# Fused decay attention and gated feed-forward on one core: block 1's v before the output weights' second half, projection 0's second half inside gate/value 1

## The chip, the cores and the metric

The kernel runs on one core of a Trainium2 chip. The metric is the device time of one execution in microseconds. Engines: TensorE (PE) multiplies matrices, VectorE (DVE), ScalarE (ACT) and GpSimd (POOL) work on tiles, and SyncE (SP), POOL and ACT issue DMAs from their own instruction streams.

## The reference

Inputs are q, k, v of 4 batches, 8 heads, 768 positions and head dimension 64, and a decay lam per head. A causal linear attention with decay runs in blocks along the sequence and carries a 64 x 64 state per batch and head. Its output, 3072 tokens by 512, goes through a gated feed-forward with 1536 inner features:

```python
intra = np.einsum('bhic,bhjc->bhij', qb, kb) * Dmask[None]
intra = np.einsum('bhij,bhjd->bhid', intra, vb)
inter = np.einsum('bhid,bhde->bhie', qb * lam_pow[None], kv_state)
out[:, :, sl] = intra + inter
kb_dec = kb * rev_pow[None]
kv_state = lam_block * kv_state + np.einsum('bhsd,bhse->bhde', kb_dec, vb)
...
gate = 1.0 / (1.0 + np.exp(-(x @ w_gate)))
return (gate * (x @ w_val)) @ w_out
```

## The kernel before, in words

The sequence is cut into six blocks (n = 0 to 5) of 128 positions. A block of all four batches gives 512 tokens. Everything is computed in bf16 with sums in PSUM.

**Attention of a block.** q and k have to lie with the head dimension on the partitions. For blocks 0 and 1 PE transposes them (`t_`, L219), and ACT and DVE evict them into KS and QS (`e_k` L240, `e_q` L226; from block 1 on, QS is also multiplied by powers of lam). From block 2 on, DMA transposes that SP issues do it (`xbar`, L251): kt first, then qt. `piece_s` (L260) computes the scores of one batch into two PSUM tiles, and `piece_m` (L271) multiplies them on DVE with the decay mask into MT. `piece_kd` (L115) makes the decayed keys on ACT, one instruction for each head and half of the batches (for block 0 one per head). `att` (L476) then runs `piece_i` (state times q; it reads Sb), `piece_a` (scores times v, into the same PSUM tiles), `piece_x` (eviction to XT; for blocks 0 and 1 batches 0 and 2 on ACT, 1 and 3 on DVE) and `piece_c` (decayed keys times v, four head pairs in two halves), whose result updates the state Sb on DVE. For block 0 the state was zero, so `piece_c(0)` is simply copied to Sb.

**Feed-forward of a block.** `piece_gv` (L331), called a gate/value step, computes 128 of the 1536 inner features: four matmuls for the gate (gp), a sigmoid on ACT, four matmuls for the value (vp), and a product on DVE into HT. A block has twelve such steps. `piece_po` (L349), the projection, multiplies HT of one batch (tt) with WO in twelve matmuls, evicts to ob (on ACT unless another engine is given) and stores with a DMA issued by SP. The projection of block 0 is done in two halves of 256 columns, of later blocks in one of 512, but for the last one of all.

**Order.** [...] A list, `plan`, holds the feed-forward units in order, and behind each unit stand smaller pieces of attention (`behind` L489 for block 0's gate/value steps, `after` L501 for its projection, `more` L509 for later blocks). In the kernel before, `piece_c(0)` stands behind gate/value step 5 of block 0; the transposes of block 1's batches 0, 1 behind step 8; those of batches 2, 3 behind projection unit 2 of the first half; block 1's kd in four groups behind projection units, the last ahead of `att(1)`, which stands behind unit 2 of the second half. `next_loads(n)` (L441) issues the DMA transposes of block n on SP, two tiny POOL copies that wait for them (`gate`), and the loads of block n's v and of the next block's k and q on POOL. For block 2 it stands behind gate/value step 2 of block 1.

**Loads.** POOL issues nearly all of them, in program order (L163 to L169 and L423 to L433); for a swapped half of the batches, `load` (L83) issues two DMAs. The order around the change is k and q of block 1's batches 2, 3, then WO's second 256 columns, then v of block 1, then k and q of block 2.

**PSUM.** Attention tiles take turns in five buffers (`ps_at`), those of the feed-forward in three (`ps_ff`). Ahead of block 0's feed-forward stand matmuls on zeros (`zeros`, L364) that fill PE's time.

Of the kernel before, what the change touches and what calls it, by code (L numbers as in the profile page):

```python
# [16 lines left out]
def kernel(  # L17
# [11 lines left out]
    nc = tc.nc  # L29

    B, H, S, D = q.shape
# [8 lines left out]
    NB2 = B // 2  # L40
# [30 lines left out]
    def swapped(n, b):  # L71
        return n > 0 and b >= NB2

    def slot(n, b, h):
        return h ^ 1 if swapped(n, b) else h

    def half(b, h):
        return (1 - h % 2) if b >= NB2 else h % 2

    def rows_of(u):  # L80
        return slice(u * 64, (u + 1) * 64)

    def load(n, what, b0=0, b1=B):  # L83
        sl = slice(n * C, (n + 1) * C)
        for c in what:
            if (c, n) not in T_:
                T_[c, n] = qkv.tile([128, B, H, D], BF16, tag=c + "b", name=c + "b",
                                      bufs=5 if c == "v" else 4)
            src = {"q": q, "k": k, "v": v}[c]
            nat = b1 if n == 0 or c == "v" else min(b1, NB2)  # L90
            if b0 < nat:
                nc.gpsimd.dma_start(  # L92
                    out=T_[c, n][:, b0:nat],
                    in_=src[b0:nat, :, sl, :].rearrange("b h s d -> s (b h) d"))
            if nat < b1:
                m = max(nat, b0)
                for u in range(2):
                    nc.gpsimd.dma_start(  # L98
                        out=T_[c, n][:, m:b1, u::2, :],
                        in_=src[m:b1, 1 - u::2, sl, :].rearrange("b h s d -> s (b h) d"))  # L100
# [11 lines left out]
    def make_kd(n):  # L112
        KD[n] = kdp.tile([128, B, H, D], BF16, tag="kd", name="kd")

    def piece_kd(n, hs):  # L115
        for h in hs:
            for bs in ((0, B),) if n == 0 else ((0, NB2), (NB2, B)):
                at = slice(*bs)
                i = slot(n, bs[0], h)
                nc.scalar.mul(KD[n][:, at, i, :], T_["k", n][:, at, i, :], kds[:, h:h + 1])  # L120
# [9 lines left out]
    Sb = stp.tile([128, HP, B, 64], BF16, tag="Sb", name="Sb")  # L130
# [88 lines left out]
    def t_(c, n, bs):  # L219
        ps = ps_at.tile([128, len(bs), HP, C], BF16, name="t" + c, tag="ps")  # L220
        for i, b in enumerate(bs):
            for hp in range(HP):
                nc.tensor.transpose(ps[:, i, hp, :], T_[c, n][:, b, 2 * hp:2 * hp + 2, :], ident)
        (tqs if c == "q" else tks)[n, bs[0]] = ps
# [15 lines left out]
    def e_k(n, bs, parts=1):  # L240
        t = trsb.tile([128, 2, HP, C], BF16, tag="KS", name="KS")
        w = len(bs) // parts
        for i in range(parts):
            nc.scalar.copy(t[:, i * w:(i + 1) * w], tks[n, bs[0]][:, i * w:(i + 1) * w])
        for i in range(len(bs)):
            KS[n, bs[i]] = t[:, i]
# [13 lines left out]
    def piece_s(n, bs):  # L260
        for b in bs:
            sp = [ps_at.tile([128, HP, C], FP32, name=f"sp{u}", tag="ps") for u in range(2)]
            for hp in range(HP):
                for u in range(2):
                    us = slice(u * 64, (u + 1) * 64)
                    nc.tensor.matmul(sp[u][:, hp, :], lhsT=KS[n, b][us, hp, :],  # L266
                                     rhs=QS[n, b][us, hp, :],
                                     start=(hp == 0), stop=(hp == HP - 1), skip_group_check=True)
            SP[n, b] = sp

    def piece_m(n, b):  # L271
        MT[n, b] = mtp.tile([128, 2, HP, C], BF16, tag="MT", name="MT")
        for u in range(2):
            nc.vector.tensor_tensor(out=MT[n, b][:, u], in0=SP[n, b][u],  # L274
                                    in1=(mask if n else mask0)[:, 1 - u if swapped(n, b) else u],
                                    op=ALU.mult)
# [31 lines left out]
    def piece_c(n, hps):  # L308
        cp = ps_at.tile([128, len(hps), B, 64], FP32, name="cp", tag="ps")
        for i, hp in enumerate(hps):  # L310
            for b in range(B):
                for w in range(2):
                    h = 2 * hp + w
                    nc.tensor.matmul(cp[rows_of(half(b, h)), i, b, :],  # L314
                                     lhsT=KD[n][:, b, slot(n, b, h), :], rhs=T_["v", n][:, b, h, :],
                                     start=(i == 0 and b == 0), stop=(i == len(hps) - 1 and b == B - 1),
                                     skip_group_check=True)
        if n == 0:
            nc.vector.tensor_copy(Sb[:, hps[0]:hps[-1] + 1], cp)
            return  # L320
        for i, hp in enumerate(hps):
            for at, d in ((slice(0, NB2), dec), (slice(NB2, B), decs)):
                nc.vector.scalar_tensor_tensor(  # L323
                    out=Sb[:, hp, at, :], in0=Sb[:, hp, at, :], scalar=d[:, hp:hp + 1],
                    in1=cp[:, i, at, :], op0=ALU.mult, op1=ALU.add)
# [38 lines left out]
    def zeros(m):  # L364
        for _ in range(m):
            nc.tensor.matmul(zps, lhsT=Sb[:, 0, 0:2, :], rhs=Sb[:, 0:2], start=True, stop=True)  # L366
# [17 lines left out]
    tables_late()  # L384
    piece_s(0, [0])
    piece_m(0, 0)
    piece_s(0, [1])
    piece_m(0, 1)
    t_("k", 0, [2, 3])
    e_k(0, [2, 3], parts=2)  # L390
    zeros(2)
    t_("q", 0, [2])
    e_q(0, [2], nc.scalar)
# [32 lines left out]
    load(1, "q", 0, 2)  # L426
    load_gv(10, 12)
    load_wo(0, 256)
    load(1, "k", 2, 4)
    load(1, "q", 2, 4)  # L430
    load_wo(256, 512)
    load(1, "v")
    load(2, "kq")  # L433

    gates = const.tile([128, 2], BF16, tag="gates")
# [19 lines left out]
    def gv(n, ft, *more):  # L455
        unit(lambda: piece_gv(n, ft), *more)

    def po(n, tt, *more, c=(0, DM), eng=nc.scalar):
        unit(lambda: piece_po(n, tt, *c, eng), *more)

    def pair(f, n, bp):
        return lambda: f(n, [2 * bp, 2 * bp + 1])

    def m_(n, b):
        return lambda: piece_m(n, b)

    def trans(n, bp):
        def go():
            bs = [2 * bp, 2 * bp + 1]
            t_("k", n, bs)  # L470
            e_k(n, bs)
            t_("q", n, bs)
            e_q(n, bs)
        return go

    def att(n):  # L476
        def go():
            piece_i(n)
            piece_a(n, range(B))
            piece_x(n, range(B))  # L480
            if n < NSTEP - 1:
                piece_c(n, [0, 1])
                piece_c(n, [2, 3])
        return go

    def kd(n, h0):
        return lambda: piece_kd(n, [h0, h0 + 1])

    behind = {ft: [] for ft in range(NFT)}  # L489
    for ft in range(4):  # L490
# [1 line left out]
    behind[0].append(swap_halves)  # L492
    behind[1].append(lambda: make_mask(0))
    behind[3].append(lambda: make_mask(1))
    behind[5] = [pair(piece_c, 0, 0), pair(piece_c, 0, 1)]
    behind[8] = [trans(1, 0)]
    behind[9] = [pair(piece_s, 1, 0), m_(1, 0)]
    behind[10] = [m_(1, 1)]
    for ft in range(NFT):
        gv(0, ft, *behind[ft])  # L500
    after = {(0, 1): [kd(1, 0)], (0, 2): [trans(1, 1)], (0, 3): [pair(piece_s, 1, 1), m_(1, 2), kd(1, 2)],  # L501
             (1, 0): [m_(1, 3), kd(1, 4)], (1, 1): [kd(1, 6)], (1, 2): [att(1)]}
    for j in range(2):
        for tt in range(B):
            po(0, tt, *after.get((j, tt), []), c=(256 * j, 256 * (j + 1)))

    for n in range(1, NSTEP):
        nx = n + 1
        more = [[] for i in range(NFT)]  # L509
        if nx < NSTEP:  # L510
            more[3] = [lambda nx=nx: e_q(nx, [0, 1])]
            more[4] = [pair(piece_s, nx, 0), m_(nx, 0)]
            more[5] = [m_(nx, 1), lambda nx=nx: e_q(nx, [2, 3])]
            more[7] = [pair(piece_s, nx, 1), m_(nx, 2)]
            more[8] = [m_(nx, 3)]
            more[11] = [att(nx)]
        if nx < NSTEP - 1:
            for i in range(4):
                more[6 + i].append(kd(nx, 2 * i))
            more[5].append(lambda nx=nx: make_kd(nx))  # L520
        if n == 1:
            more[4:11] = more[3:10]
            more[3] = []
            more[2].append(lambda: next_loads(2))
            more[8].append(lambda: next_loads(3))
        for ft in range(NFT):
            gv(n, ft, *more[ft])
        for tt in range(B):
            if n == NSTEP - 1 and tt == B - 1:
                po(n, tt, c=(0, 256))  # L530
                po(n, tt, c=(256, 512), eng=nc.vector)
            else:
                more = [lambda n=n: next_loads(n + 3)] if tt == B - 1 and n + 3 < NSTEP else []
                po(n, tt, *more)
# [35 lines left out]
```

## Time and profile before

| | |
|---|---|
| three runs | 229.17, 229.33, 229.39 us; median 229.33 |
| the profiled execution | 229.37 us, its span 227.6 us |
| granted PE clock | 0.997 |
| PE, DVE, ACT, POOL busy | 216.2, 101.6, 100.9, 59.5 us |
| bytes moved by DMA | 25.31 MB |
| gate/value 0 starts on PE | 16.08 us |
| projection 0 starts | 39.30 us |
| gate/value 1 starts | 55.07 us |
| projection 1 starts | 79.29 us |

The profile is one execution with the start and end of each instruction. PE, DVE, ACT and POOL are busy where they work on data; time before an instruction in which its engine stood idle is given with what ended it. DMA issues on POOL and SP are listed with the time from issue to landing. Times are counted from the start of the span, so the profiled execution's own time is 1.77 us more than its last time.

### The profile page before, as it was taken

What the parts mean: (1) busy time and instruction counts of PE and PEld (TensorE: products, weight loads), DVE (VectorE), ACT (ScalarE), POOL (GpSimd) and SP (SyncE); (2) the same over time, 40 slices, a digit from 0 to 9 for tenths busy, and PEclk for the clock granted to TensorE, in tenths of its full rate; (3) what the DMA queues carried; (4) which work ended last, traced back from release to release, by engine and by line L of the source; (5) the groups of instructions that cost most, each with busy time, mean ns of one, the idle gap of its engine ahead of it and who ended that gap; (6) DMA issues with size and microseconds to landing.
All of it is one profiled execution on the core that took longest, in us unless ns stands there. A gap on an engine that the chain in (4) does not pass through costs nothing.

```text
span 227.6 us, 4227 instructions
## 1 busy us (share of the span) xinstructions
PE 216.2 (95%) x1689; PEld 110.9 (49%) x1713; DVE 101.6 (45%) x186; ACT 100.9 (44%) x216; POOL 59.5 (26%) x75
## 2 busy tenths in 40 slices
PE   6689999979999999999999999999999999999994
PEld 1444454867444644444544444554444544444443
DVE  4754657145468620388430378530368600333300
ACT  5767443565337732338532328532333342333221
POOL 7997654700067009302900030000000000000000
PEclk9999999999999999999999999999999999999998
DMA  7999999999939999995995939012100012100022
GB/s 115 147 174 200 193 180 181 194 193 178 212 57 153 147 209 106 207 193 98 109 157 154 192 53 82 0 49 92 46 3 0 0 49 92 46 0 3 0 94 92
DMA packets 106195, 25.31 MB, mean 111 GB/s; under 512 B 94144, under 2 KB 103744, under 8 KB 106176
## 3 DMA queue, kind: packets, MB, share of 16 engines
q0 software_dynamic: 82816, 13.90, 79.3%
q1 hardware_dynamic: 22896, 11.01, 19.5%
q8 instruction: 13, 0.21, 0.4%
q10 hardware_dynamic: 464, 0.14, 0.3%
q14 instruction: 6, 0.05, 0.1%
HBM read 28.32 MB, written 6.29 MB: 152 GB/s over the span
## 4 chain that ended last, share of the span: by engine, by line
PE 77%; DMA 15%; POOL 5%; issue 2%; DVE 0%; POOLq 0%
PE po L354 25%; PE vp L342 23%; PE gp L336 22%; DMA WO<-in_moe_w_out_dram 7%; DMA qb<-in_q_dram 5%; DMA WG<-in_moe_w_gate_dram 3%; PE op L296 2%; PE sp L266 2%; PE op L285 1%; POOL vb L92 1%; POOL kb L92 1%; PE cp L314 1%; POOL WG L104 1%; POOL qb L92 1%; POOL WV L105 1%
## 5 line engine op out<-in xcount | busy, mean ns | idle before, releaser
L345 DVE TENSOR_TENSOR ht<-sg,vp 128x512 bf16<-128x512 bf16 x72 | 49.4, 686 | 94.3 <-PE vp L342 92.7
L342 PE MATMUL vp<-XT,WV 128*128 128x512 bf16 x287 | 73.8, 379 | 0.3
L336 PE MATMUL gp<-XT,WG 128*128 128x512 bf16 x272 | 71.5, 379 | 1.5 <-issue 0.8
L339 ACT ACTIVATE sg<-gp 128x512 bf16<-128x512 f32 x72 | 43.0, 597 | 66.5 <-PE gp L336 63.0
L354 PE MATMUL po<-WO,ht 128*128 128x512 bf16 (+1 forms) x343 | 63.6, 342 | 1.8 <-DMA WO<-in_moe_w_out_dram 1.5
L354 PEld LDWEIGHTS <-ht 128*128 128x128 bf16 x348 | 33.5, 98 | 29.8 <-issue 1.5
L342 PEld LDWEIGHTS <-WV 128*128 128x128 bf16 x288 | 28.2, 98 | 34.0 <-DMA WV<-in_moe_w_val_dram 0.2
L336 PEld LDWEIGHTS <-WG 128*128 128x128 bf16 x288 | 27.3, 98 | 32.4 <-issue 0.3
L357 ACT COPY ob<-po 128x512 f32<-128x512 f32 (+1 forms) x28 | 14.4, 515 | 45.3 <-PE po L354 45.3
L274 DVE TENSOR_TENSOR MT<-sp,mask 128x512 bf16<-128x512 f32 x48 | 30.5, 682 | 1.9 <-PE sp L266 1.9
L120 ACT ACTIVATE kd<-kb,kds 128x128 bf16<-128x128 bf16 (+1 forms) x72 | 23.8, 402 | 0.0
L439 POOL COPY gates<-kt 128x1 bf16<-128x1 bf16 x4 | 0.7, 186 | 54.8 <-DMA kt<-kb 54.8
L306 ACT CAST XT<-op 128x512 bf16<-128x512 f32 x21 | 10.9, 597 | 5.6 <-PE op L296 5.6
L92 POOL DMA_DIRECT2D vb<-in_v_dram x7 | 10.9, 1563 | 1.4 <-issue 0.9
L323 DVE SCALAR_TENSOR_TENSOR Sb<-Sb,dec,cp 128x128 bf16<-128x128 bf16 x32 | 8.6, 342 | 3.3 <-PE cp L314 3.3
L98 POOL DMA_DIRECT2D kb<-in_k_dram x10 | 8.8, 895 | 3.2 <-DMA WO<-in_moe_w_out_dram 2.3
L98 POOL DMA_DIRECT2D qb<-in_q_dram x10 | 8.9, 918 | 1.3 <-DMA kb<-in_k_dram 0.8
L92 POOL DMA_DIRECT2D qb<-in_q_dram x7 | 8.4, 1205 | 0.8 <-POOLq L554 0.8
L366 PE MATMUL zps<-Sb 128*128 128x512 bf16 x19 | 6.5, 469 | 1.6 <-DVE Sb L147 1.5
L92 POOL DMA_DIRECT2D kb<-in_k_dram x6 | 6.9, 1158 | 1.4 <-DMA WV<-in_moe_w_val_dram 0.8
L296 PE MATMUL op<-MT,vb 128*64 128x128 bf16 x184 | 6.5, 221 | 0.0
L296 PEld LDWEIGHTS <-vb 128*64 128x64 bf16 x184 | 5.3, 110 | 1.3 <-issue 0.4
(55 smaller groups left out, 81.9 us busy)
## 6 DMA issues: line engine op xcount, KB each, us to landing
out_dram<-ob SPq DMA_DIRECT2D x19, 256.0 KB, 2.0
vb<-in_v_dram POOLq DMA_DIRECT2D x5, 512.0 KB, 7.0
qb<-in_q_dram POOLq DMA_DIRECT2D x7, 256.0 KB, 8.3
kb<-in_k_dram POOLq DMA_DIRECT2D x6, 256.0 KB, 8.0
WO<-in_moe_w_out_dram POOLq DMA_DIRECT2D x2, 768.0 KB, 14.6
WG<-in_moe_w_gate_dram POOLq DMA_DIRECT2D x5, 256.0 KB, 9.2
WV<-in_moe_w_val_dram POOLq DMA_DIRECT2D x5, 256.0 KB, 9.8
kb<-in_k_dram POOLq DMA_DIRECT2D x10, 128.0 KB, 8.6
```

What stands on the lines that cost most here:

```text
L92: nc.gpsimd.dma_start(out=T_[c, n][:, b0:nat], in_=src[b0:nat, :, sl, :].rearrange("b h s d -> s (b h) d"))
L98: nc.gpsimd.dma_start(out=T_[c, n][:, m:b1, u::2, :], in_=src[m:b1, 1 - u::2, sl, :].rearrange("b h s d -> s (b h) d"))
L120: nc.scalar.mul(KD[n][:, at, i, :], T_["k", n][:, at, i, :], kds[:, h:h + 1])
L274: nc.vector.tensor_tensor(out=MT[n, b][:, u], in0=SP[n, b][u], in1=(mask if n else mask0)[:, 1 - u if swapped(n, b) else u], op=ALU.mult)
L296: nc.tensor.matmul(OP[n, b][rows_of(w), hp, :], lhsT=T_["v", n][:, b, h, :], rhs=MT[n, b][:, slot(n, b, h) % 2, hp, :], start=(n == 0 and ...
L306: (e.tensor_copy if e is nc.vector else e.copy)(XT[n][:, :, b, :], OP[n, b])
L336: nc.tensor.matmul(gp, lhsT=WG[:, mt, fs], rhs=x[:, mt, :], start=(mt == 0), stop=(mt == NMT - 1))
L339: nc.scalar.activation(sg, gp, AF.Sigmoid)
L342: nc.tensor.matmul(vp, lhsT=WV[:, mt, fs], rhs=x[:, mt, :], start=(mt == 0), stop=(mt == NMT - 1))
L345: nc.vector.tensor_mul(HT[n, ft], sg, vp)
L354: nc.tensor.matmul(po[:, :c1 - c0], lhsT=HT[n, ft][:, tt * 128:(tt + 1) * 128], rhs=WO[:, ft, c0:c1], start=(ft == 0), stop=(ft == NFT - 1))
L357: (eng.copy if eng is nc.scalar else eng.tensor_copy)(o, po[:, :c1 - c0])
```

## The change

Five parts. In the prologue of block 0, the PE transposes of k for batches 2, 3 and their eviction come ahead of batch 1's scores. `piece_c(0)` moves from behind gate/value step 5 to behind projection unit 3 of block 0, just ahead of `att(1)`, and its copies to Sb run on ACT instead of DVE. Block 1's k and q of batches 2 and 3 are loaded, transposed and evicted one batch at a time, and v of block 1 is loaded ahead of WO's second half. Of block 1's kd, the half for batches 0, 1 moves behind gate/value steps 10 and 11; the half for batches 2, 3 is eight instructions ahead of `att(1)`. The second half of projection 0 (four units) is done between gate/value steps 1 and 2 of block 1. At the very end, the last 256 columns of the last projection are computed, evicted and stored as two pieces of 128, the first evicted on DVE, the second on ACT.

```diff
--- before.py
+++ after.py
@@ -112,9 +112,9 @@
     def make_kd(n):
         KD[n] = kdp.tile([128, B, H, D], BF16, tag="kd", name="kd")
 
-    def piece_kd(n, hs):
+    def piece_kd(n, hs, parts=(0, 1)):
         for h in hs:
-            for bs in ((0, B),) if n == 0 else ((0, NB2), (NB2, B)):
+            for bs in ((0, B),) if n == 0 else [((0, NB2), (NB2, B))[i] for i in parts]:
                 at = slice(*bs)
                 i = slot(n, bs[0], h)
                 nc.scalar.mul(KD[n][:, at, i, :], T_["k", n][:, at, i, :], kds[:, h:h + 1])
@@ -316,7 +316,7 @@
                                      start=(i == 0 and b == 0), stop=(i == len(hps) - 1 and b == B - 1),
                                      skip_group_check=True)
         if n == 0:
-            nc.vector.tensor_copy(Sb[:, hps[0]:hps[-1] + 1], cp)
+            nc.scalar.copy(Sb[:, hps[0]:hps[-1] + 1], cp)
             return
         for i, hp in enumerate(hps):
             for at, d in ((slice(0, NB2), dec), (slice(NB2, B), decs)):
@@ -384,10 +384,10 @@
     tables_late()
     piece_s(0, [0])
     piece_m(0, 0)
+    t_("k", 0, [2, 3])
+    e_k(0, [2, 3], parts=2)
     piece_s(0, [1])
     piece_m(0, 1)
-    t_("k", 0, [2, 3])
-    e_k(0, [2, 3], parts=2)
     zeros(2)
     t_("q", 0, [2])
     e_q(0, [2], nc.scalar)
@@ -426,10 +426,11 @@
     load(1, "q", 0, 2)
     load_gv(10, 12)
     load_wo(0, 256)
-    load(1, "k", 2, 4)
-    load(1, "q", 2, 4)
+    for b in range(2, 4):
+        load(1, "k", b, b + 1)
+        load(1, "q", b, b + 1)
+    load(1, "v")
     load_wo(256, 512)
-    load(1, "v")
     load(2, "kq")
 
     gates = const.tile([128, 2], BF16, tag="gates")
@@ -464,9 +465,8 @@
     def m_(n, b):
         return lambda: piece_m(n, b)
 
-    def trans(n, bp):
+    def trans(n, bs):
         def go():
-            bs = [2 * bp, 2 * bp + 1]
             t_("k", n, bs)
             e_k(n, bs)
             t_("q", n, bs)
@@ -483,8 +483,11 @@
                 piece_c(n, [2, 3])
         return go
 
-    def kd(n, h0):
-        return lambda: piece_kd(n, [h0, h0 + 1])
+    def kd(n, h0, h1=None, **kw):
+        return lambda: piece_kd(n, range(h0, h1 or h0 + 2), **kw)
+
+    def s_(n, b):
+        return lambda: piece_s(n, [b])
 
     behind = {ft: [] for ft in range(NFT)}
     for ft in range(4):
@@ -492,17 +495,18 @@
     behind[0].append(swap_halves)
     behind[1].append(lambda: make_mask(0))
     behind[3].append(lambda: make_mask(1))
-    behind[5] = [pair(piece_c, 0, 0), pair(piece_c, 0, 1)]
-    behind[8] = [trans(1, 0)]
+    behind[8] = [trans(1, [0, 1])]
     behind[9] = [pair(piece_s, 1, 0), m_(1, 0)]
-    behind[10] = [m_(1, 1)]
+    behind[10] = [m_(1, 1), kd(1, 0, 4, parts=[0])]
+    behind[11] = [kd(1, 4, 8, parts=[0])]
     for ft in range(NFT):
         gv(0, ft, *behind[ft])
-    after = {(0, 1): [kd(1, 0)], (0, 2): [trans(1, 1)], (0, 3): [pair(piece_s, 1, 1), m_(1, 2), kd(1, 2)],
-             (1, 0): [m_(1, 3), kd(1, 4)], (1, 1): [kd(1, 6)], (1, 2): [att(1)]}
-    for j in range(2):
-        for tt in range(B):
-            po(0, tt, *after.get((j, tt), []), c=(256 * j, 256 * (j + 1)))
+    cols = [(256 * j, 256 * j + 256) for j in range(2)]
+    po(0, 0, c=cols[0])
+    po(0, 1, trans(1, [2]), c=cols[0])
+    po(0, 2, s_(1, 2), m_(1, 2), trans(1, [3]), c=cols[0])
+    po(0, 3, s_(1, 3), m_(1, 3), pair(piece_c, 0, 0), pair(piece_c, 0, 1), kd(1, 0, 8, parts=[1]),
+       att(1), c=cols[0])
 
     for n in range(1, NSTEP):
         nx = n + 1
@@ -525,10 +529,14 @@
             more[8].append(lambda: next_loads(3))
         for ft in range(NFT):
             gv(n, ft, *more[ft])
+            if (n, ft) == (1, 1):
+                for tt in range(B):
+                    po(0, tt, c=cols[1])
         for tt in range(B):
             if n == NSTEP - 1 and tt == B - 1:
                 po(n, tt, c=(0, 256))
-                po(n, tt, c=(256, 512), eng=nc.vector)
+                po(n, tt, c=(256, 384), eng=nc.vector)
+                po(n, tt, c=(384, 512))
             else:
                 more = [lambda n=n: next_loads(n + 3)] if tt == B - 1 and n + 3 < NSTEP else []
                 po(n, tt, *more)
```

## The prediction

> **What bounds the kernel now.** I read the page's busy line first, then TensorE's (PE's) timeline, then the timelines of the engines that feed it. The busy line:
>
> ```profile
> PE 216.2 (95%) x1689; PEld 110.9 (49%) x1713; DVE 101.6 (45%) x186; ACT 100.9 (44%) x216; POOL 59.5 (26%) x75
> ```
>
> PE is busy 216.2 of 227.6 us, so a change can win only where PE stands idle, and every new idle stretch is lost in full, since nothing behind it has slack. PE's timeline around the change (start, length, instruction, idle time before it):
>
> ```profile
> 26.57 0.69 PE L314 MATMUL cp<-vb,kd 128*64 128x64 bf16 x32
> ...
> 39.30 4.11 PE L354 MATMUL po<-WO,ht 128*128 128x256 bf16 x36
> ...
> 47.63 4.09 PE L354 MATMUL po<-WO,ht 128*128 128x256 bf16 x36 [1.48 <-DMA WO<-in_moe_w_out_dram]
> 51.66 0.64 PE L285 MATMUL op<-QS,Sb 64*64 64x128 bf16 x32
> 52.23 1.08 PE L296 MATMUL op<-MT,vb 128*64 128x128 bf16 x32
> 53.14 0.67 PE L314 MATMUL cp<-vb,kd 128*64 128x64 bf16 x32
> ...
> 65.52 0.62 PE L266 MATMUL sp<-QS,kt 64*128 64x128 bf16 x16
> ```
>
> The one wait worth removing is 1.48 us at 47.63, for the second half of the output weights (WO). A second gate shows no idle time: WO's first half lands at 39.25 (issued 24.95, 14.3 us to landing), just as PE comes to projection 0 at 39.30. PE cannot start it sooner whatever is taken out of gate/value 0. GpSimd's (POOL's) timeline shows the queue discipline:
>
> ```profile
> 24.95 1.02 POOL L108 DMA_DIRECT2D WO<-in_moe_w_out_dram  x1 [0.39 <-DMA WG<-in_moe_w_gate_dram]
> ...
> 39.54 0.87 POOL L98 DMA_DIRECT2D kb<-in_k_dram  x1 [2.27 <-DMA WO<-in_moe_w_out_dram]
> ```
>
> The load at 39.54 is the eighth after WO's first half and waits for its landing; the other POOL waits here also point eight loads back. ScalarE (ACT), VectorE (DVE) and the SP queue:
>
> ```profile
> 50.84 1.27 ACT L120 ACTIVATE kd<-kb,kds 128x128 bf16<-128x128 bf16 x4
> 52.02 0.35 ACT L357 COPY ob<-po 128x256 f32<-128x256 f32 x1
> 52.68 1.07 ACT L306 CAST XT<-op 128x512 bf16<-128x512 f32 x2 [0.31 <-PE op L296]
> ```
> ```profile
> 64.58 0.69 DVE L233 TENSOR_TENSOR QS<-qt,lamq 128x1024 bf16<-128x1024 bf16 x1
> ```
> ```profile
> 56.17 3.92 SPq L254 DMA_TRANSPOSE kt<-kb  x1
> 60.27 1.89 SPq L254 DMA_TRANSPOSE qt<-qb  x1
> ...
> 125.62 1.90 SPq L254 DMA_TRANSPOSE kt<-kb  x1
> 127.73 2.26 SPq L254 DMA_TRANSPOSE qt<-qb  x1
> ```
>
> kd is done on ACT before attention 1 begins to be evicted. And block 2's transposed q lands at 64.57 (60.27 plus 4.3), DVE takes it at 64.58, PE needs the result at 65.52: this path has about 0.2 us of slack.
>
> [...] The trace agrees (kd, ob and XT above run in program order), and this decides the forecast. [...] The trace has 390 and, from four in 1.27 to 1.28 us, 297. [...] So a transpose queued on SP behind a store waits for that store's eviction; the trace agrees (161.6 us of waits of SP's stores for ob).
>
> **The change part by part.** The sum is against the profiled execution: 229.37 us, span 227.6, 1.77 around it (the median is 229.33). Pitches on PE from the starts above: a 256-column projection of 12 matmuls 1.31 (36 in 3.94); k and q transposes of one batch 0.45; scores of one batch 0.28; piece_i 0.57, piece_a 0.91, piece_c pair 0.61; a gate/value step 1.727.
>
> *Prologue order.* Batches 2, 3 of k are transposed inside a 0.47 us PE gap. QS of batch 2 still waits for q's DMA (PE idle 0.49 at 11.16), so nothing is gained; a loss up to 0.4 would vanish in the next point's slack. 0.
>
> *piece_c of block 0 leaves gate/value 0.* PE would end that stage about 0.6 early and wait at 39.30 for WO. Gain 0. The same work returns after the anchor: +0.61.
>
> *Loads.* Eight small k/q loads replace four, and each POOL issue costs about 0.73 (the price of a load with as few packets, WG's 0.74) against 0.87. The eighth starts at 39.54 behind WO, v at 40.3, WO's second half at 42.0. v takes 6.9 to landing when the queue is empty (the one at 65.25), so it lands at 47.2; WO2 lands 4.95 later (its distance from q's landing before, 42.6 to 47.55), at 52.2. Batch 2's k, q are there by 40.9 (needed 41.9), batch 3's by 43.6 (needed 44.0 to 44.2). The 1.48 goes, and neither v nor WO2 is late, with about 1 and 2.3 us to spare.
>
> *Projection 0, first half, with attention between.* From 39.30: po 0 to 40.61, po 1 to 41.93, transposes to 42.37, po 2 to 43.69, scores 2 to 43.97, transposes to 44.41, po 3 to 45.73. DVE does the mask product of batch 2 from 44.12 (two at a pitch of 0.60) and QS of batch 3 by about 45.72; scores 3 run 45.78 to 46.06, piece_c(0) to 46.67.
> *First new wait.* Until now piece_c(0)'s Sb copies were hidden 25 us ahead; now attention 1 needs them at once. ACT copies Sb from 46.60 (0.22 after its matmuls, as XT does) and, at a pitch of 0.49, has the second at 47.67. DVE's mask product of batch 3 runs 46.21 to 47.50, and piece_i's third matmul needs its PSUM buffer (five, in rotation). piece_i starts at 47.56: 0.9 idle. It ends at 48.17, piece_a at 49.08 (v there at 47.2), the first piece_c half at 49.38.
> *Second new wait.* Behind the Sb copies on ACT stand eight kd, 8 x 0.297 = 2.38, from 47.58 to 49.96, and only then the two XT evictions of batches 0, 2: to 50.54 and 51.04. The second piece_c half needs the last kd and batch 0's PSUM buffer: 50.6. Gate/value 1 needs all of XT: 51.10. Idle 1.2 plus 0.2. Before, 1.32 us of projection covered XT's eviction; that cover is gone. The two kd groups moved into gate/value 0 cost nothing (0.6 + 1.27 us of ACT per 1.73 step, the excess of 0.1 hidden under projection 0).
>
> *Second half inside gate/value 1.* Two steps to 54.55, four projections to 59.80; ACT's evictions (0.37 each per 1.31) are covered. Before, the same work was done at 58.52. So **+1.28**: 1.48 and little else won, 0.61 paid back, 2.3 newly idle.
>
> *What that does to SP.* The first transpose of block 2 stands behind the last of these stores. Before, PE left the projection at 55.07 and kt was issued at 56.17, 1.10 later; now at 60.90. Before, block 2's q landed 8.7 us after the large load ahead of it (51.7 to 60.4), with a transpose crossing; now that makes 60.9 at the latest, so the pair goes through unhindered. The trace has this once, at 125.62: kt's issue to qt's landing 6.9 us. The others took 8.0 to 8.4, with q still loading. I take 6.9: qt lands at 67.8, DVE's QS ends at 68.5, PE's scores of block 2 start at 68.6 rather than 65.52. PE comes there at 59.80 + 4 x 1.727 = 66.7: a **third new wait of 1.9**. After it everything is the old schedule, later by 3.1; block 3's loads and transposes shift along, with 10 us in hand.
>
> *Tail.* The last 256 columns go as two of 128: the final eviction falls from DVE's 0.42 to about 0.26 on ACT (585 and 366 ns at 512 and 256 columns, continued), the store from 128 to 64 KB, unpriced: 0 to 0.3. 24 matmuls at 0.056 (the transposes' pitch) cost 0.02 more. Taken -0.15; ends -0.4 and +0.1.
>
> Sum: scores of block 2 at 68.6 against 65.52 is 3.08 later, that is 1.28 and 1.9 less a gap of 0.1 that was there before: 229.37 + 3.08 - 0.15 = **232.3**.
>
> **Rivals.** *Transposes slow:* the pair takes 8.2, as three of four did, because loads or stores cross it: 233.6. For: it is the commoner value. Against: k and q of block 2 should be in by then. 13%.
> *Only the first wait is real:* ACT's kd do not hold XT (1.4 us less): kt at 59.5, qt at 66.4, scores at 67.2: 230.9. [...] 13%.
> *Faster:* attention stays fed, as it does now at 51.66 to 55.07, because the six evicting steps fit under PE's work. Then PE works 18.1 us through, projection 0 ends at 57.4, 1.1 ahead of before, and with the tail gives 228.1. It decides only if the transposes, issued at 58.5, land within 5.0 us; beyond 6.25 the kernel is slower even so, and the shortest pair seen is 6.9. 5%.
> *v or WO2 late by over 2 us:* above 234. 5%. *Gains and losses cancel:* 229.3. 2%.
>
> **How the numbers follow.** Forecast 62%. The range takes in the two middle rivals: 230.7 to 233.8, some 88%, and part of the forecast's own spread. About 0.2% is what a measurement here can tell from no change; beyond it slower 93%, faster 5%, within it 2%.
>
> **What would show it.** Right: PE's line for WO at 47.63 without a wait; idle before op L285 of about 0.9 and before gate/value 1 of over 1 us with ACT's kd in one row of eight ahead of XT; kt issued near 60.9, QS of block 2 near 67.8 and an idle time of about 1.9 before sp L266. Wrong: XT evicted ahead of kd; kt issued before the last store of projection 0; or qt landing before 65.

## The result, and the profile after

The changed kernel takes 232.48 us (median of 4 runs, 232.10 to 232.85) against 229.35 for the kernel before (4 runs, 229.17 to 229.39): 1.0138 times as long, 95% interval 1.0120 to 1.0156. The forecast was 232.3, range 230.7 to 233.8. The profiled execution of the changed kernel took 232.10 us with a span of 230.3, against 229.37 and 227.6: 2.73 us more.

The busy line of the page after: PE has more busy time than before and the same share. A share of 95% says nothing of where the loss lies. Nor can the two times be subtracted: before, 24 of the 1713 matmuls have no record (1689 beside 1713 weight loads), after, none of 1725.

```profile
PE 219.7 (95%) x1725; PEld 111.6 (48%) x1725; DVE 100.6 (44%) x185; ACT 102.6 (45%) x220; POOL 61.6 (27%) x79
```

PE's timeline after (start, length, instruction, idle time before it and what ended it) shows each place of the forecast:

```profile
39.22 2.79 PE L354 MATMUL po<-WO,ht 128*128 128x256 bf16 x24 [0.67 <-DMA WO<-in_moe_w_out_dram]
...
46.22 0.70 PE L314 MATMUL cp<-vb,kd 128*64 128x64 bf16 x32
47.34 1.02 PE L285 MATMUL op<-QS,Sb 64*64 64x128 bf16 x32 [0.43 <-ACT Sb L319]
48.51 1.08 PE L296 MATMUL op<-MT,vb 128*64 128x128 bf16 x32
49.43 0.98 PE L314 MATMUL cp<-vb,kd 128*64 128x64 bf16 x32
51.12 1.02 PE L336 MATMUL gp<-XT,WG 128*128 128x512 bf16 x4 [0.70 <-ACT XT L306]
...
54.56 5.40 PE L354 MATMUL po<-WO,ht 128*128 128x256 bf16 x48
...
68.59 0.62 PE L266 MATMUL sp<-QS,kt 64*128 64x128 bf16 x16 [1.72 <-DVE QS L233]
```

The old wait of 1.48 us for WO's second half is gone: at 54.56 there is no idle time. In its place stand a wait of 0.67 ahead of projection 0 (most of it the time that piece_c(0) left behind), idle time in and around attention 1, 0.70 before gate/value 1, and 1.72 before the scores of block 2. Waits can also hide inside a line that merges several instructions: the 32 matmuls of piece_i take 1.02 us where they took 0.64, those of piece_c 0.98 where they took 0.67.

ACT's timeline after shows the row that holds XT up: the Sb copies, eight kd, then the evictions to XT.

```profile
46.71 1.07 ACT L319 CAST Sb<-cp 128x512 bf16<-128x512 f32 x2 [0.34 <-PE cp L314]
47.67 2.45 ACT L120 ACTIVATE kd<-kb,kds 128x128 bf16<-128x128 bf16 x8
50.01 1.05 ACT L306 CAST XT<-op 128x512 bf16<-128x512 f32 x2
```

Both transposes on SP's queue, and DVE's use of the result 0.1 us after its landing (63.12 plus 4.6):

```profile
60.91 2.03 SPq L254 DMA_TRANSPOSE kt<-kb  x1
63.12 2.40 SPq L254 DMA_TRANSPOSE qt<-qb  x1
```
```profile
67.85 0.69 DVE L233 TENSOR_TENSOR QS<-qt,lamq 128x1024 bf16<-128x1024 bf16 x1 [1.90 <-DMA qt<-qb]
```

### The profile page after: what moved, and what is told of

It reads as the page before. It is cut to its first block, busy times and chain, and to the rows that moved or that the text cites. A ratio compares the mean times of both kernels' runs of the same rounds, so it can differ in the third digit from the quotient of the medians.

```text
span 230.3 us, 4287 instructions
## 1 busy us (share of the span) xinstructions
PE 219.7 (95%) x1725; PEld 111.6 (48%) x1725; DVE 100.6 (44%) x185; ACT 102.6 (45%) x220; POOL 61.6 (27%) x79
## 4 chain that ended last, share of the span: by engine, by line
PE 76%; DMA 15%; POOL 3%; ACT 2%; issue 1%; SPq 1%; DVE 0%; POOLq 0%; DVEq 0%; ACTq 0%
PE po L354 27%; PE gp L336 21%; PE vp L342 21%; DMA WO<-in_moe_w_out_dram 6%; DMA WG<-in_moe_w_gate_dram 4%; DMA vb<-in_v_dram 3%; PE sp L266 2%; DMA qt<-qb 2%; PE op L296 2%; ACT kd L120 1%; PE op L285 1%; SPq L254 1%; PE cp L314 1%; POOL qb L92 1%; POOL vb L92 1%
## 5 line engine op out<-in xcount | busy, mean ns | idle before, releaser
L336 PE MATMUL gp<-XT,WG 128*128 128x512 bf16 x288 | 74.0, 379 | 1.1 <-ACT XT L306 0.7
L354 PE MATMUL po<-WO,ht 128*128 128x512 bf16 (+2 forms) x360 | 63.9, 337 | 0.7 <-DMA WO<-in_moe_w_out_dram 0.7
L357 ACT COPY ob<-po 128x512 f32<-128x512 f32 (+2 forms) x29 | 14.8, 509 | 47.8 <-PE po L354 47.8
L98 POOL DMA_DIRECT2D qb<-in_q_dram x12 | 10.2, 864 | 5.8 <-DMA WO<-in_moe_w_out_dram 3.7
L98 POOL DMA_DIRECT2D kb<-in_k_dram x12 | 10.1, 850 | 2.4 <-DMA WG<-in_moe_w_gate_dram 1.2
L366 PE MATMUL zps<-Sb 128*128 128x512 bf16 x21 | 7.5, 484 | 1.5 <-DVE Sb L147 1.5
L92 POOL DMA_DIRECT2D qb<-in_q_dram x7 | 8.4, 1205 | 0.9 <-POOLq L562 0.8
L92 POOL DMA_DIRECT2D kb<-in_k_dram x6 | 6.9, 1157 | 0.8 <-DMA WG<-in_moe_w_gate_dram 0.8
L266 PE MATMUL sp<-QS,kt 64*128 64x128 bf16 x128 | 5.0, 217 | 1.7 <-DVE QS L233 1.7
```

The costliest lines, as they stand in the source:

```text
L92: nc.gpsimd.dma_start(out=T_[c, n][:, b0:nat], in_=src[b0:nat, :, sl, :].rearrange("b h s d -> s (b h) d"))
L98: nc.gpsimd.dma_start(out=T_[c, n][:, m:b1, u::2, :], in_=src[m:b1, 1 - u::2, sl, :].rearrange("b h s d -> s (b h) d"))
L336: nc.tensor.matmul(gp, lhsT=WG[:, mt, fs], rhs=x[:, mt, :], start=(mt == 0), stop=(mt == NMT - 1))
L354: nc.tensor.matmul(po[:, :c1 - c0], lhsT=HT[n, ft][:, tt * 128:(tt + 1) * 128], rhs=WO[:, ft, c0:c1], start=(ft == 0), stop=(ft == NFT - 1))
L357: (eng.copy if eng is nc.scalar else eng.tensor_copy)(o, po[:, :c1 - c0])
```

## The experiments

The theory: three waits take the place of the one removed. State copies of block 0 and kd stand on ACT ahead of XT, and block 2's transposes stand on SP behind the stores of projection 0's second half. The main rival: the place in the queues costs nothing, and loads or transposes are late by themselves. All kernels but one are edits of the changed kernel, and all are compared with the kernel before on the same chip (medians 229.28 or 229.29 us).

**Transposes first.** Edit:

```diff
-            more[2].append(lambda: next_loads(2))
+            more[1].append(lambda: next_loads(2))
```

> The changed kernel, but block 2's DMA transposes are issued by SP before the stores of projection 0's second half (behind gate/value step 1 of block 1 instead of step 2). Theory (SP holds the transposes behind the last store, and this costs 1.7 us of PE time at 68.59): kt is issued near 57.5, when k of block 2 has landed, qt's data are there by 62, the wait before the scores of block 2 falls from 1.72 to at most 0.5 us, and the time from 232.1 to 230.5 (230.2 to 230.9), slower than before by some 0.5%. Rival (the transposes themselves or their loads are late, not their place in the queue): qt still lands after 67, the wait stays at 1.5 us or more, time 231.9 to 232.6.

Measured: 230.40 us (230.34 to 230.81), ratio 1.0054 (1.0042 to 1.0066). SP's queue and PE's line in this kernel:

```profile
57.47 3.15 SPq L254 DMA_TRANSPOSE kt<-kb  x1
61.01 1.37 SPq L254 DMA_TRANSPOSE qt<-qb  x1
62.48 2.71 SPq L358 DMA_DIRECT2D out_dram<-ob  x4
```
```profile
66.93 0.62 PE L266 MATMUL sp<-QS,kt 64*128 64x128 bf16 x16
```

kt is issued 3.4 us sooner, the stores follow it, and the scores of block 2 start without a wait. This one place in the order on SP is worth 1.7 us between the profiled executions and 2.1 between medians. The third wait is shown. One part of the theory missed: qt landed at 65.4 (61.01 plus 4.4), not by 62. The pair took 7.9 us here, and that was still in time.

**The kd in earlier gaps of ACT.** Edit:

```diff
-    po(0, 1, trans(1, [2]), c=cols[0])
-    po(0, 2, s_(1, 2), m_(1, 2), trans(1, [3]), c=cols[0])
-    po(0, 3, s_(1, 3), m_(1, 3), pair(piece_c, 0, 0), pair(piece_c, 0, 1), kd(1, 0, 8, parts=[1]),
+    po(0, 1, trans(1, [2]), kd(1, 0, 4, parts=[1]), c=cols[0])
+    po(0, 2, s_(1, 2), m_(1, 2), trans(1, [3]), kd(1, 4, 8, parts=[1]), c=cols[0])
+    po(0, 3, s_(1, 3), m_(1, 3), pair(piece_c, 0, 0), pair(piece_c, 0, 1),
```

> The changed kernel, but the eight kd of batches 2, 3 run in two groups of four in gaps of ScalarE, behind the transposes of batch 2 and of batch 3, instead of in one row ahead of the XT evictions. Theory (kd in the FIFO ahead of XT causes the second wait, but v's landing at 48.4 and VectorE's XT of batch 3, which ends at 50.5, come next): gate/value 1 starts at 50.5 instead of 51.12; time lower by 0.6, that is 231.5 (231.2 to 231.9). Rival (the whole second wait of over 1 us is won, as the prediction priced it): gate/value 1 at 49.8 or earlier, time 230.8. Rival (kd hides nothing, the queue order does not matter): no change, 232.1 to 232.5.

Measured: 232.31 us, ratio 1.0142 (1.0111 to 1.0173); six runs, four from 231.82 to 232.66 and two at 234.3. The time alone would speak for the rival "no change". PE's timeline of the profiled run (one of the two) says why:

```profile
39.49 2.79 PE L354 MATMUL po<-WO,ht 128*128 128x256 bf16 x24 [0.84 <-DMA WO<-in_moe_w_out_dram]
...
50.84 1.04 PE L336 MATMUL gp<-XT,WG 128*128 128x512 bf16 x3 [0.44 <-DVE XT L306]
...
69.18 0.62 PE L266 MATMUL sp<-QS,kt 64*128 64x128 bf16 x16 [2.57 <-DVE QS L233]
...
71.12 1.91 PE L342 MATMUL vp<-XT,WV 128*128 128x512 bf16 x4 [0.22 <-issue]
```
```profile
60.65 3.12 SPq L254 DMA_TRANSPOSE kt<-kb  x1
63.95 1.98 SPq L254 DMA_TRANSPOSE qt<-qb  x1
```

From the start of projection 0 to gate/value 1 it is 11.35 us instead of 11.90: the 0.55 are won. Of these 0.27 go to the later start of projection 0 in this execution (39.49). The rest reaches SP: kt is issued 0.26 us sooner than after the change (60.65). But the pair of transposes took 7.6 us from kt's issue to qt's landing (63.95 plus 4.3) instead of 6.8, and so PE waits longer for it. The last line of PE is a surprise, taken up below: four value matmuls took 1.91 us after the long wait, where they took 1.03 after the change (at 70.02). Both losses are seen in this execution. The four runs that are not near 234 have a median of 231.92, 0.56 below the changed kernel and at the edge of the theory's range, and three of them are faster than every run of the changed kernel. So the gain is not lost as a rule: kt stands behind the stores and moves with them.

**State copies back in gate/value 0.** Edit:

```diff
-            nc.scalar.copy(Sb[:, hps[0]:hps[-1] + 1], cp)
+            nc.vector.tensor_copy(Sb[:, hps[0]:hps[-1] + 1], cp)
...
+    behind[5] = [pair(piece_c, 0, 0), pair(piece_c, 0, 1)]
...
-    po(0, 3, s_(1, 3), m_(1, 3), pair(piece_c, 0, 0), pair(piece_c, 0, 1), kd(1, 0, 8, parts=[1]),
+    po(0, 3, s_(1, 3), m_(1, 3), kd(1, 0, 8, parts=[1]),
```

> The changed kernel, but piece_c of block 0 and its copies to Sb are back behind gate/value step 5, on VectorE. Theory (the first wait and 0.6 us of matmuls after the anchor go, but v's landing is then late by itself): projection 0 still starts at 39.2, piece_i starts near 46.2 and piece_a waits for v until 48.4; the kd end a microsecond sooner, gate/value 1 starts at 50.5 instead of 51.12, time lower by 0.6: 231.5 (231.2 to 231.9). Rival (no other wait stands behind the state copies): gate/value 1 starts at 49.6, lower by 1.5: 230.6.

Measured: 233.12 us (232.60 to 233.75), ratio 1.0169 (1.0155 to 1.0184): a miss for both. PE's timeline:

```profile
47.40 0.60 PE L285 MATMUL op<-QS,Sb 64*64 64x128 bf16 x29 [0.60 <-DVE MT L274]
48.34 1.08 PE L296 MATMUL op<-MT,vb 128*64 128x128 bf16 x32 [0.34 <-DMA vb<-in_v_dram]
...
50.36 1.04 PE L336 MATMUL gp<-XT,WG 128*128 128x512 bf16 x3 [0.37 <-DVE XT L306]
...
68.68 0.62 PE L266 MATMUL sp<-QS,kt 64*128 64x128 bf16 x16 [2.10 <-DVE QS L233]
```

In attention 1 it is as expected: v is the latest at piece_a, and gate/value 1 starts 0.8 sooner than after the change, though projection 0 started at 39.55 and not at 39.2. The first line shows what stands beside the state copies: with them gone, piece_i waits 0.60 us for DVE's mask product of batch 3 all the same. Of the 0.8 us, 0.3 reach the second half of projection 0 (54.26 instead of 54.56), because PE waits 0.27 there for WO's second half, and kt is issued 0.29 sooner (60.62). The pair of transposes then took 7.1 us instead of 6.8, so that the scores of block 2 start at 68.68 instead of 68.59. The profiled run is 1.0 us slower than that of the changed kernel (the medians differ by 0.6), and nearly all of it lies elsewhere: from the end of the last eviction to the end of the span 3.59 us pass, in the changed kernel 2.68; the last store took 2.5 us to landing instead of 1.6. Why this store lands later here was not found.

**The kd early, with the transposes first.** Both edits above together.

> The changed kernel with block 2's transposes ahead of the second half's stores and with the kd of batches 2, 3 in earlier gaps of ScalarE. Theory (the second wait was really shortened by 0.6 us when the kd were moved alone, but the wait for block 2's transposes swallowed it): with that wait gone the 0.6 us show in the time, 229.8 (229.5 to 230.1) against 230.4 with the transposes alone. Rival (moving the kd wins nothing): 230.4.

Measured: 230.03 us (229.74 to 230.83), ratio 1.0039 (1.0026 to 1.0052): 0.37 less than with the transposes alone, in the theory's range but not all of its 0.6. PE's timeline shows where the rest stays:

```profile
50.41 1.04 PE L336 MATMUL gp<-XT,WG 128*128 128x512 bf16 x3 [0.44 <-DVE XT L306]
...
54.38 5.42 PE L354 MATMUL po<-WO,ht 128*128 128x256 bf16 x48 [0.34 <-DMA WO<-in_moe_w_out_dram]
```

From projection 0's start (39.24) to gate/value 1 it is 11.17 us, 0.73 less than after the change; 0.34 of it goes to a wait for WO's second half, which lands at 54.3 here (issued 42.02, 12.3 to landing; 53.7 in the changed kernel).

**All three.** Transposes first, kd early, state copies back.

> The changed kernel with three parts undone or moved: block 2's transposes ahead of the second half's stores, the kd in earlier gaps, and piece_c of block 0 with its copies back behind gate/value step 5 on VectorE. Theory (v's landing at 48.3 is now the latest, so state copies and kd together win no more than either did): gate/value 1 starts at 50.4, time 229.7 (229.4 to 230.0), still not faster than before. Rival (the waits add up): gate/value 1 starts at 49.5 or earlier, 228.8.

Measured: 230.74 us (229.76 to 231.13), ratio 1.0061 (1.0046 to 1.0076). The profiled run took 229.76, and its timeline has the theory's gate/value start:

```profile
48.54 1.08 PE L296 MATMUL op<-MT,vb 128*64 128x128 bf16 x32 [0.91 <-DMA vb<-in_v_dram]
...
50.57 1.04 PE L336 MATMUL gp<-XT,WG 128*128 128x512 bf16 x3 [0.44 <-DVE XT L306]
```

The waits don't add up: v, landing at 48.5, now holds attention by itself. But the median of 230.74 lies outside the theory's range, a miss, and above the 230.03 of the kernel that leaves the state copies where the change put them. To see where the other runs lose time, the same kernel was run again:

> The kernel with three parts undone once more, the same text: its profiled run was 229.76 but five others 230.7 to 231.1, most at a granted clock of 0.997 to 0.998. Theory (a wait for v of block 1, with the waits around it, sometimes lowers the granted PE clock): a profile of a slower run shows the clock below 1.0 in the stretch from 46 to 60 us and matmuls longer than 216 ns there. Rival (loads land later in those runs): the clock is 1.0 throughout and gate/value 1 or the scores of block 2 start 0.7 to 1.0 later.

Measured: 230.89 us, ratio 1.0071 (1.0056 to 1.0086). In the profile of a run of 231.03 the clock was 1.00 in every stretch of PE work, so the theory falls. The scores of block 2 started at 66.68 instead of 66.28 (0.31 of it a wait for WO's second half), and 0.9 us came at the end: 3.59 us from the last eviction's end to the span's end, as in the kernel with the state copies back. The first part is the rival's kind, late loads, with 0.4 us instead of its 0.7 to 1.0. The late end (the last store took 2.4 us to landing) stays open.

**Four loads instead of eight.** All three, and the loads of batches 2, 3 together again; transposes of both batches behind projection unit 1 (`trans23` does them and their evictions):

```diff
-    for b in range(2, 4):
-        load(1, "k", b, b + 1)
-        load(1, "q", b, b + 1)
+    load(1, "k", 2, 4)
+    load(1, "q", 2, 4)
     load(1, "v")
...
+    po(0, 1, trans23, kd(1, 0, 4, parts=[1]), c=cols[0])
+    po(0, 2, s_(1, 2), m_(1, 2), s_(1, 3), m_(1, 3), kd(1, 4, 8, parts=[1]), c=cols[0])
+    po(0, 3, att(1), c=cols[0])
```

> As the kernel with three parts undone, but batches 2, 3 of block 1 are loaded together again (four loads, not eight) and transposed behind projection unit 1. Theory (with eight loads, the eighth waits on POOL for WO's first half, and v stands behind it: v issued at 40.3, the DMA queue empty for over a microsecond): v is issued near 32.7, lands at 46.8 instead of 48.4, WO's second half at 51.7; gate/value 1 starts at 49.2, the scores of block 2 near 65.1; time 228.6 (228.3 to 229.0), faster than before. Rival (v's place does not matter, the mask products on VectorE or the evictions hold attention 1): gate/value 1 at 50.2 or later, 229.5.

Measured: 228.64 us (228.23 to 228.81), ratio 0.9972 (0.9961 to 0.9983): faster than the kernel before. POOL's and PE's timelines:

```profile
33.10 1.68 POOL L92 DMA_DIRECT2D vb<-in_v_dram  x1 [1.14 <-DMA qb<-in_q_dram]
34.77 1.02 POOL L108 DMA_DIRECT2D WO<-in_moe_w_out_dram  x1
...
39.53 0.88 POOL L98 DMA_DIRECT2D kb<-in_k_dram  x1 [2.59 <-DMA WO<-in_moe_w_out_dram]
```
```profile
49.58 1.04 PE L336 MATMUL gp<-XT,WG 128*128 128x512 bf16 x3 [0.44 <-DVE XT L306]
...
65.29 0.62 PE L266 MATMUL sp<-QS,kt 64*128 64x128 bf16 x16
```

In the changed kernel POOL stood as follows:

```profile
39.45 0.74 POOL L98 DMA_DIRECT2D qb<-in_q_dram  x1 [3.70 <-DMA WO<-in_moe_w_out_dram]
40.33 1.69 POOL L92 DMA_DIRECT2D vb<-in_v_dram  x1
42.00 1.03 POOL L108 DMA_DIRECT2D WO<-in_moe_w_out_dram  x1
```

In both traces the load that is eighth after WO's first half waits for it: POOL stood 3.70 us until 39.45 in the changed kernel, 2.59 until 39.53 here. With eight small loads that is the last q, and v stands behind it; with four it is a load of block 2, and v went out 7 us sooner and landed at 46.5 instead of 48.4. So the split into single batches cost v 1.9 us of the lead that the new order gave it. The edit also moves the transposes and scores: v's wait of 0.91 us is gone, and piece_i's wait for DVE's mask product falls from 0.60 to 0.16. Between the profiled executions all of it is worth 1.0 us (229.76 to 228.76); the 2.1 between medians may contain late ends like the one that stayed open.

**The same, block 2 one step later.** `more` of block 1 moved on by one more gate/value step.

> As the kernel with four loads, but all pieces of block 2 stand one more gate/value step later behind block 1. Theory: the remaining wait for block 2's transposed q, at most 0.5 us, goes; time equal to the one with four loads or up to 0.4 lower, 228.4. Rival (attention 2, now with its last kd right ahead, is late at the end of gate/value 1): 0.5 or more slower than with four loads.

Measured: 228.73 us (228.32 to 228.84), ratio 0.9976 (0.9967 to 0.9985). No difference from the kernel with four loads: there was no wait left to remove.

**The tail alone,** in the kernel before:

```diff
-                po(n, tt, c=(256, 512), eng=nc.vector)
+                po(n, tt, c=(256, 384), eng=nc.vector)
+                po(n, tt, c=(384, 512))
```

> The kernel before with only the last 256 columns of the last projection split in two pieces of 128, the second evicted on ScalarE. Theory from the trace of the changed kernel (from the last projection's first matmul to the end 13.57 us against 13.94): faster by 0.37, 229.0 (ratio 0.998 to 0.9988). Rival (the prediction's size): faster by 0.15, 229.2. Rival (nothing): 229.35.

Measured: 229.06 us (21 runs) against 229.29, ratio 0.9992 (0.9985 to 0.9998): a gain of 0.23. The traces before and after had shown 0.37, more than the runs bear out (the interval reaches from 0.05 to 0.34).

**Filling the wait.** The kernel with kd early, and eight matmuls without use ahead of the scores of block 2 (they are extra work, their sum is read by nobody):

```diff
+    def filler():
+        zz = ps_ff.tile([128, DM], FP32, name="zz", tag="ff")
+        for _ in range(8):
+            nc.tensor.matmul(zz, lhsT=ident, rhs=WG[:, 0, 0:512], start=True, stop=True)
...
+            more[5].insert(0, filler)
```

> The changed kernel with the kd in earlier gaps, and eight added matmuls of 512 columns, whose result nobody reads, ahead of the scores of block 2, 8 x 0.216 = 1.7 us of PE work inside the wait of 2.6. Theory (the two runs at 234.3 come from the granted PE clock, which fell to 0.52 after PE had been idle for 2.57 us): with PE idle for under 1 us the clock stays at 1.0, no run lies near 234, median 231.9 (231.6 to 232.3). Rival (the clock falls for another reason): runs near 234 stay.

Measured: 231.76 us (231.46 to 232.36), ratio 1.0114 (1.0096 to 1.0133), no run near 234:

```profile
66.11 1.89 PE L495 MATMUL zz<-WG,ident 128*128 128x512 bf16 x8
68.17 0.62 PE L266 MATMUL sp<-QS,kt 64*128 64x128 bf16 x16 [0.17 <-DVE QS L233]
```

The median is in the theory's range. Four runs are few, though: if one run in three is slow, as it was without the filler (two of six), four in a row without a slow one come about one time in five. The trace also shows the gain of the early kd behind attention: kt is issued at 60.30, 0.6 us sooner than after the change, the pair takes 6.9 us, and the scores of block 2 start 0.42 sooner (68.17 instead of 68.59).

## Why the prediction was right, point by point

*Prologue order:* forecast 0. It did win something, gate/value 0 starts at 15.84 instead of 16.08, but this went into the wait for WO ahead of projection 0.

*Anchor of projection 0:* forecast 39.30, gain 0 from the earlier end of gate/value 0. Measured 39.22 with a wait of 0.67 for WO. Right.

*Loads:* v was put at 47.2 and WO's second half at 52.2; they came at 48.4 and 53.7 (42.00 plus 11.7). The mis-sized term is v's time to landing, taken from a load with empty queues, 6.9 us; here it took 8.1. Neither cost PE time in the changed kernel, because the kd row held PE until 51.12 anyway. The "1 and 2.3 us to spare" were really less than nothing for v (piece_a began at 48.51 instead of 48.17) and 0.9 for WO. The experiments had to pay for that: v was next in line when the state copies or the kd were moved.

*First wait:* 0.9 us forecast before piece_i. The trace has 0.43 before it and 0.38 more inside its 32 matmuls. Only a part of it is due to the state copies: with them moved back, 0.60 was left for DVE's mask product. *Second wait:* gate/value 1 at 51.10 forecast, 51.12 measured, but the sign that the prediction named, over 1 us idle before it, was not there: it was 0.70, with 0.31 more inside piece_c. From piece_c(0) to gate/value 1 PE lost 2.2 us in all (4.90 from 46.22 to 51.12, less 2.70 of work at the prediction's pitches), where 2.3 were forecast. In the trace ACT ran the eight kd (from 47.67, 2.45 us in all, 390 ns for one; 2.38 forecast) ahead of XT (from 50.01). That this order causes the second wait is shown by moving the kd; but only 0.55 to 0.79 could be won by that, not the 1.4 that the rival "only the first wait is real" set on it, since v and DVE's eviction of batch 3 come next.

*Second half and SP:* projection done at 59.80 forecast and measured (next matmul of PE), kt at 60.9 and 60.91, the scores of block 2 at 68.6 and 68.59. The pair took 6.8 (60.91 to 67.7) where 6.9 was taken from the one unhindered pair (its lines give 6.8: 125.62 to 127.73 plus 4.7). The mechanism is shown by the transposes moved ahead of the stores: kt was issued at 57.47, and PE's wait of 1.72 us was gone.

*Tail:* -0.15 forecast, -0.23 measured alone.

*Sum:* 3.08 - 0.15 = 2.93 forecast; 2.73 between the two profiled executions, 3.13 between the medians. The runs of the changed kernel spread over 0.75 us, those of the kernel before over 0.22. A likely source, argued and not shown, is the pair of transposes: 6.8, 7.6, 7.1 and 6.9 us in the four profiles where it stands behind the stores (after the change, kd early, state copies back, filled), and there it is on the path. The last load of block 2's q landed 0.2, 1.3, 0.8 and 0.8 us after kt's issue in these profiles. So that the pair went through unhindered held only just: q was put at 60.9 at the latest and landed at 61.1, with kt issued at 60.91. To hit the total within 0.2 us took some luck there.

*Rivals.* "Transposes slow" was not the changed kernel's case, though 7.6 did occur. "Faster" failed where the forecast put its point: attention did not stay fed, and even with all three parts undone the kernel took 230.74. It became faster only when v also came sooner and batch 3's scores with it, at 228.64; against the tail alone, 229.06, that leaves 0.42 for the new order of loads and work.

## What to carry to other kernels

When a wait is removed by moving work, list on every engine and DMA queue what the moved work now stands ahead of: here ACT's XT and SP's transposes paid, not the part that was edited. A time that does not move says little until the trace shows where the gain stopped; two repairs of one stage can each be worth over half a microsecond, together no more than one of them, and a transfer behind the stage that happens to take longer (here the pair of transposes, 7.6 us instead of 6.8) can hide them in one execution. And where one load waits for an earlier one to land, splitting loads between them can push what stands behind past that wait: here the last small q waited 3.70 us for WO's first half, eight loads before it, and v, behind it, was issued at 40.33 instead of 33.10.

## What the runs showed of the hardware

After the long wait for block 2 PE ran slower, at a granted clock of 0.52 and then 0.63. In the profiled run of the kernel with kd early, the stretches after the wait of 2.57 us (columns: stretch, length, busy time and count of PE, PEld, DVE, ACT, POOL, granted clock, DMA share, GB/s):

```profile
68.00:70.00 2.00, 0.82 (x18) 0.63 (x19) 1.66 (x3) 0.00 (x0) 1.49 (x2) 1.00 0.00 0
70.00:72.00 2.00, 1.78 (x6) 0.69 (x6) 0.89 (x2) 0.60 (x1) 2.00 (x3) 0.52 0.59 38
72.00:74.00 2.00, 2.00 (x7) 0.78 (x6) 0.86 (x2) 0.00 (x0) 2.00 (x3) 0.63 2.39 153
```

From the first to the second scores of block 2 it took 7.53 us instead of 5.84 (69.18 to 76.71, and 68.59 to 74.43), 1.7 us more. The clock accounts for it: 0.48 and 0.37 of two stretches of 2 us are missing, 1.7 us. It happened in two of six runs, if the other run at 234.3, whose mean clock was 0.993 too, is counted; with filler it happened in none of four (mean clock 0.998 to 1.000), and after waits of 1.72 and 2.10 us (the changed kernel, state copies back) the clock was 1.00 in the stretches from 68 to 74 us. That the wait is the cause fits all of this, but so few runs do not show it, nor what sets the two runs of six apart.
